# Loading queries and keys threefold and splitting them in place, in a kernel of one attention and two feed-forward stages

## The chip, the cores and the metric

The kernel runs on one core of one Trainium2 chip. The metric is the device time of one execution in microseconds (us). Five engines work side by side, each through its own instructions in order: TensorE (PE, with its weight loads PEld), VectorE (DVE), ScalarE (ACT), GpSimd (POOL), and SyncE (SP), which here only issues DMA transfers. An engine that reaches an instruction whose inputs are missing waits, and everything behind that instruction on the same engine waits with it.

## The reference

Inputs are q, k, v and o_gate (4 batches, 8 heads, 768 steps, 40 numbers a head) and two gates a step and head. For each batch and head a 40 by 40 state is carried over the 768 steps:

```python
m_new  = max(f_t + m, i_t)
f_stab = exp(f_t + m - m_new);  i_stab = exp(i_t - m_new)
C = f_stab * C + i_stab * outer(v_t, k_t)
n = f_stab * n + i_stab * k_t
y_t = sigmoid(o_t) * (C @ q_t) / max(|n . q_t|, 1)
```

The result, 3072 rows of 320, goes through two layers: `h = max(x@w1, x@w2, x@w3)` of width 768 and `h@w_out`; then `h = x@w_in` of width 2048, `g = h*clip(h+3, 0, 6)/6`, and `g@w_out`. Everything is float32. The weights come to the kernel as float64 numbers seen as int64.

## The kernel before

**Stages.** Stage 1 is attention with the first layer, stage 2 the second layer. Attention is cut into 24 groups: a group g is one batch and one chunk of 128 steps, all 8 heads (`attention(g)`, line 415). Groups 0 to 7 (g < GF = 8) are called early groups here, 8 to 23 late ones (the change's title counts them from 1). The first layer takes the groups in blocks of 2, 2 and five times 4 (BLK1), so its products (lines 284, 817, 819; tiles h and acc) run between the attention steps of later groups. Stage 2 (lines 930 to 1028) takes six blocks of 4 groups, and 16 slices k of its weights; a product into pi (line 284, called in g_in), then ACT, DVE, ACT and POOL steps (984 to 988), then products into po (1002 to 1004).

**Precision.** A product of float32 numbers is made as several products of rounded parts. A matrix x is split into hi, x rounded by a copy, and lo = x - hi. In the late groups queries and keys lie in a tile qs of 120 rows, three times 40: the rows of the queries are hi, hi, lo and those of the keys hi, lo, hi (or the same with the roles swapped), so that one product over 120 rows sums hi*hi, hi*lo and lo*hi. The state that the queries meet lies likewise in a tile cs of 120 rows.

**How a late group's qs is made.** Line 434 loads queries and keys once, 320 KB, into raw, a tile of 128 rows that has no regard to heads (raw has one buffer). ACT copies it to hi (sq, line 455), POOL subtracts to lo (sl, 458), SP writes both to a tensor qs_d in the chip's DRAM (sw, 464; 640 KB), and five more transfers (sr, 471, 473, 474; 960 KB) read it back into the rows of qs. The first of these steps waits for the product pv of the group AHEAD = 5 groups before.

**How the state's cs is made.** After the state cn of a group is there (line 705), ACT copies it to ch (709), POOL subtracts to cl (713), and six small transfers (cd, 720) put cl, ch and ch into the rows of cs. The product `in` (567) reads cs and qs.

**Weights of stage 1.** 24 pieces (`weights(k, p)`, line 732), each of 384 or 320 KB: SP loads it (wl, line 739, through load_f64, 246 to 249; four buffers wr), ACT reads its bytes twice (rebase 255, tail 263), DVE joins the two (267), ACT rounds (752), POOL subtracts (274). Both ACT steps read raw and so end the use of the buffer.

**Order.** Stage 1's steps are put to a planner (class Plan, 120). Each step is given an engine, a duration, a priority and what it reads and writes; the planner plays them through and writes each engine's order down. MOVED adds to the priority of single steps by their number, GP is the priority of the gates of chunks 1 to 5 and WP0, WPR that of the weights. SP's order comes from the same plan, so a transfer that must wait for a buffer holds up all that stand behind it on SP. Up to three PSUM tiles pa serve attention, two tiles h the first layer's inputs.

**Between the stages.** Each block of stage 1 writes its result x2 into x2_d in DRAM (xd, 850), two transfers a group; stage 2 reads it back likewise (x_load, 952).

Of the kernel before, what the change touches and what calls it, by code (L numbers as in the profile page):

```python
# [21 lines left out]
L = 128  # L22
# [4 lines left out]
QF = 2 * D * H * L // 128  # L27
FF1, FF2 = 768, 2048
K1, K2 = FF1 // 128, FF2 // 128
DP = 42  # L30
# [6 lines left out]
AHEAD, WP0, WPR = 5, 500, 100  # L37
GP, NSG = 1900, 4
GPB, GGB = 3, 4
PE_, PM, PC = 0, 2 * 10**6, 3 * 10**6  # L40

MOVED = {
    135: -1449, 206: -3641, 217: -1367, 319: 149, 371: 268, 387: 4201, 480: 39, 517: 2678, 522: 1135,
    539: 1040, 553: -4154, 559: -4352, 565: -156, 594: 613, 659: -1758, 707: -7, 715: 420, 742: -3344,
    940: 2702, 941: 5996, 953: 4436,
# [4 lines left out]
    qs=2, raw=1, sp=1, kvo=2, kvg=2, fd=2, vt=2, vw=2, nm=2, rr=2, y=2, sg=2, ct=1, cn=B + 1, ch=1, cl=1, cs=B + 1,  # L50
# [69 lines left out]
class Plan:  # L120
# [22 lines left out]
    def order(p):  # L143
# [17 lines left out]
        while ready:  # L161
            best = None
            for n in ready:
                o = p.ops[n]
                s = at[o["eng"]]
                for d in o["deps"]:
                    x = p.ops[d]
                    end = done[d]
                    if x["eng"] != o["eng"] or x["eng"] == "SP":
                        end += p.LAT.get(x["eng"], 0) + o["wait"]  # L170
                    s = max(s, end)
# [34 lines left out]
            if o["eng"] == "SP":  # L206
                dma = max(dma, s) + o["size"] / 210
                end = dma + 2000
# [16 lines left out]
def body(tc, ctx, qk0, qkf, kvo, ig, fg, w1, w2, out):  # L225
# [11 lines left out]
    qs_d = [dram.tile([2, 2, D, H * L], F32, name=f"qs_d{g}") for g in range(GF, G)]  # L237
    x2_d = [dram.tile([128, 3, L], F32, name=f"x2_d{g}") for g in range(G)]
# [7 lines left out]
    def load_f64(src, name):  # L246
        t = stg.tile([128, WC], I64, tag="wr", name=f"raw{name}", bufs=BUFS["wr"])[:, 0:src.shape[-1]]
        nc.sync.dma_start(t, src)
# [41 lines left out]
    with ExitStack() as c1:  # L290
# [14 lines left out]
        idt = cs1.tile([128, NC_, 2, BH], F32, name="idt")  # L305
        dL = cs1.tile([128, NC_ - 1, BH // 2], F32, name="dL")
        junk = cs1.tile([128, 512], BF16, name="junk")
# [4 lines left out]
        def gates(gp1, c0, c1_, pr):  # L312
# [71 lines left out]
            P.add("SP", 120, pr, load, w=[F, I], size=2 * 4 * w * BH)  # L384
# [30 lines left out]
        def attention(g):  # L415
# [7 lines left out]
            QS, FD, KVO = ("qs", g), [("fd", g, a) for a in range(2)], ("kvg" if g < 2 else "kvo", g)  # L423
# [3 lines left out]
            def lq():  # L427
# [16 lines left out]
            if g < GF:  # L444
                P.add("SP", 120, pr - 2100, lq, w=[QS], size=4 * 40 * 2048)
            else:
                P.add("SP", 60, pr - 4000, lq, r=[("pv", g - AHEAD)], w=[("raw", g)], size=4 * 128 * QF)
            P.add("SP", 60, pr - 2000, lk, w=[KVO], size=4 * 128 * 976)

            if g >= GF:  # L450
                d = qs_d[g - GF]

                def sq():
                    s["sp"] = sb("sp", g, [128, 2, QF], F32R)
                    nc.scalar.copy(s["sp"][:, 0], s["raw"])

                def sl():
                    nc.gpsimd.tensor_tensor(
                        out=s["sp"][:, 1], in0=s["raw"], in1=s["sp"][:, 0].bitcast(F32), op=ALU.subtract
                    )  # L460


                def sw():
                    nc.sync.dma_start(
                        d.rearrange("z a d n -> z (a d n)").rearrange("z (p f) -> p z f", f=QF), s["sp"].bitcast(F32)
                    )

                def sr():
                    s["qs"] = q = sb("qs", g, [120, 2, H, L], F32R)
                    q = q.bitcast(F32).rearrange("p a h t -> p a (h t)")  # L470
                    nc.sync.dma_start(q[0:D], d[0].rearrange("a d n -> d a n"))
                    for r, (zq, zk) in enumerate(((0, 1), (1, 0)), 1):
# [608 lines left out]
```

## Time and profile before

| | |
|---|---|
| median of 3 runs | 793.09 us (789.65 to 795.54) |
| profiled execution, its own time | 792.57 us |
| span from its first to its last instruction | 790.8 us |
| mean granted clock of TensorE | 0.956 |
| PE busy | 757.2 us (96%) |
| DVE, ACT, POOL busy | 400.6, 309.2, 423.3 us |
| moved by DMA | 92.65 MB |

The profile comes from one execution. It gives the busy time of each engine, in all and in slices of the span, the granted clock of TensorE (1.00 is 2.4 GHz, 0.50 is 1.2 GHz), and the waits, each put down to the event that came last before the engine went on. A busy PE need not work at its peak.

### The profile page before, as it was taken

The numbers are of one execution on the slowest core, as the hardware profiler recorded it, in microseconds if no ns is written. First come the engines' busy times: TensorE is split into PE (matmuls) and PEld (weight loads), VectorE is DVE, ScalarE is ACT, GpSimd is POOL, SyncE is SP. The second block draws the span as 40 slices with busy tenths as digits, with TensorE's granted clock in tenths as the row PEclk, the third lists the DMA queues.
The fourth block names the chain that finished last, engine by engine and source line by source line (L and its number), as shares of the span: only waits on it lengthen the run. The fifth ranks groups of instructions, "written<-read, shape, count | busy, mean of one in ns | idle before, by whom it ended". The sixth has DMA issues, their size and how long they took to land.

```text
span 790.8 us, 13152 instructions
## 1 busy us (share of the span) xinstructions
PE 757.2 (96%) x5063; PEld 661.8 (84%) x5063; DVE 400.6 (51%) x618; ACT 309.2 (39%) x597; POOL 423.3 (54%) x388
## 2 busy tenths in 40 slices
PE   8878969899999998999999999999999999999997
PEld 6768869788888787888888878898998899898986
DVE  5987738668868776578425665312212113121210
ACT  4585422222223122222415886634433334433432
POOL 3788737757768687573514456535334334333331
PEclk7689679999999999999999999999999999999999
DMA  8578567675657758743322642200100000000000
GB/s 260 164 242 273 162 170 200 161 239 178 199 175 212 228 158 246 233 148 84 112 59 76 202 157 72 68 1 10 59 1 0 34 1 1 34 1 1 34 1 34
DMA packets 52078, 92.65 MB, mean 117 GB/s; under 512 B 6032, under 2 KB 28528, under 8 KB 52016
## 3 DMA queue, kind: packets, MB, share of 16 engines
q1 hardware_dynamic: 52016, 91.82, 38.2%
q8 instruction: 40, 0.66, 0.3%
q14 instruction: 22, 0.18, 0.1%
HBM read 70.78 MB, written 18.43 MB: 113 GB/s over the span
## 4 chain that ended last, share of the span: by engine, by line
PE 60%; DMA 11%; ACT 5%; DVE 4%; POOL 4%; SPq 3%; issue 2%; POOLq 0%; ACTq 0%; DVEq 0%
PE pi L284 20%; PE h L284 13%; PE po L1003 6%; PE po L1002 6%; PE po L1004 6%; DMA qs<-qs_d 4%; PE acc L817 3%; DMA raw<-in_w 2%; DMA qs_d<-sp 2%; SPq L720 2%; DVE t L267 2%; PE sc L536 1%; DMA fd<-f_d 1%; ACT a L255 1%; PE acc L819 1%
## 5 line engine op out<-in xcount | busy, mean ns | idle before, releaser
L284 PE MATMUL h<-x,w 128*128 128x512 f32 (+1 forms) x1008 | 224.8, 374 | 6.7 <-ACT m L785 6.7
L988 POOL TENSOR_TENSOR gg<-r,gg 128x512 fp32r<-128x512 f32 x96 | 125.6, 1318 | 184.4 <-ACT gg L987 174.3
L284 PEld LDWEIGHTS h<-x,w 128*128 128x128 f32 x1008 | 175.7, 198 | 36.3 <-ACT m L785 8.1
L284 PE MATMUL pi<-xs,w 128*128 128x512 f32 x768 | 193.0, 395 | 1.5 <-ACT w L946 0.8
L985 DVE SCALAR_TENSOR_TENSOR r<-r,pi 128x512 f32<-128x512 f32 x96 | 64.3, 686 | 230.3 <-ACT r L984 230.1
L284 PEld LDWEIGHTS pi<-xs,w 128*128 128x128 f32 x768 | 140.8, 188 | 29.7 <-ACT w L946 1.1
L1002 PE MATMUL po<-w,gg 128*128 128x320 f32 x384 | 118.3, 310 | 1.1 <-ACT gg L987 0.5
L1003 PE MATMUL po<-w,gg 128*128 128x320 f32 x384 | 118.0, 309 | 0.0
L984 ACT ACTIVATE r<-pi,b 128x512 f32<-128x512 f32 x96 | 64.0, 687 | 133.8 <-PE pi L284 133.2
L1004 PE MATMUL po<-w,gg 128*128 128x320 f32 x384 | 111.2, 309 | 0.0
L801 POOL TENSOR_TENSOR hh<-m,hh 128x512 fp32r<-128x512 f32 (+1 forms) x42 | 51.1, 1216 | 70.2 <-ACT hh L797 68.9
L787 DVE TENSOR_TENSOR m<-h,m 128x512 f32<-128x512 f32 (+1 forms) x84 | 50.9, 606 | 63.6 <-PE h L284 51.2
L1002 PEld LDWEIGHTS po<-w,gg 128*128 128x128 f32 x384 | 72.1, 188 | 5.7 <-ACT gg L987 1.5
L817 PE MATMUL acc<-hh,w 128*128 128x512 f32 (+1 forms) x252 | 76.5, 382 | 0.0
L1003 PEld LDWEIGHTS po<-w,gg 128*128 128x128 f32 x384 | 72.1, 188 | 3.0
L987 ACT CAST gg<-r 128x512 fp32r<-128x512 f32 x96 | 59.0, 621 | 36.6 <-DVE r L985 34.4
L797 ACT CAST hh<-m 128x512 fp32r<-128x512 f32 (+1 forms) x42 | 23.5, 559 | 125.7 <-PE acc L817 117.2
L1004 PEld LDWEIGHTS po<-w,gg 128*128 128x128 f32 x384 | 70.4, 188 | 1.0 <-POOL gg L988 0.2
L274 POOL TENSOR_TENSOR w<-t,w 128x384 fp32r<-128x384 f32 (+2 forms) x46 | 49.0, 1073 | 22.0 <-ACT w L946 11.5
L506 DVE TENSOR_TENSOR_SCAN fd<-fd,ident 128x512 f32<-128x512 f32 x40 | 58.1, 1462 | 2.5 <-DMA fd<-f_d 2.5
L267 DVE SCALAR_TENSOR_TENSOR t<-a,t 128x384 uint32<-128x384 uint32 (+1 forms) x56 | 46.0, 840 | 15.6 <-ACT t L263 14.0
L817 PEld LDWEIGHTS acc<-hh,w 128*128 128x128 f32 x252 | 47.0, 200 | 6.3
(107 smaller groups left out, 971.9 us busy)
## 6 DMA issues: line engine op xcount, KB each, us to landing
raw<-in_w SPq DMA_DIRECT2D x34, 384.0 KB
kvo<-in_kvo SPq DMA_DIRECT2D x22, 488.0 KB
fd<-f_d SPq DMA_DIRECT2D x20, 512.0 KB
qs_d<-sp SPq DMA_DIRECT2D x16, 640.0 KB
qs<-qs_d SPq DMA_DIRECT2D x64, 160.0 KB
raw<-in_w SPq DMA_DIRECT2D x22, 320.0 KB
raw<-in_qkf SPq DMA_DIRECT2D x16, 320.0 KB
qs<-qs_d SPq DMA_DIRECT2D x16, 320.0 KB
```

The source lines that it names most:

```text
L267: nc.vector.scalar_tensor_tensor(out=t, in0=a.bitcast(U32), scalar=3, in1=t, op0=ALU.logical_shift_left, op1=ALU.bitwise_or)
L284: nc.tensor.matmul(ps, wt[:, a:a + 128], x[:, r], start=n == 0, stop=n == len(order) - 1)
L506: nc.vector.tensor_tensor_scan(out=half, data0=s.get(("bc", a), half), data1=ident4.rearrange("p h t -> p (h t)"), initial=0.0, op0=ALU.mu ...
L801: nc.gpsimd.tensor_tensor(out=t[:, 1], in0=T["m", j, k], in1=t[:, 0].bitcast(F32), op=ALU.subtract)
L817: nc.tensor.matmul(acc[a], wo[:, a * 128:128 + a * 128], h, start=first, stop=last)
L984: nc.scalar.activation(r, ps, AF.Relu, bias=b3)
L985: nc.vector.scalar_tensor_tensor(out=r, in0=r, scalar=6.0, in1=ps, op0=ALU.min, op1=ALU.mult)
L987: nc.scalar.copy(gg[:, 0], r)
L988: nc.gpsimd.tensor_tensor(out=gg[:, 1], in0=r, in1=gg[:, 0].bitcast(F32), op=ALU.subtract)
L1002: nc.tensor.matmul(po[t], hi, wo[:, 0:320], start=first, stop=False)
L1003: nc.tensor.matmul(po[t], hi, wo[:, 320:640], start=False, stop=False)
L1004: nc.tensor.matmul(po[t], lo, wo[:, 0:320], start=False, stop=last)
```

## The change

- A late group loads queries (a = 0) and keys (a = 1) from the inputs into two tiles raw of 120 rows, three transfers of 40 rows each (160 KB), six in all. raw has 2 buffers. The tensor qs_d, its write and its reads are gone.
- `hm`: ACT multiplies raw by a column `lows`, 1 in the rows that are to hold lo and 0 in the others, and rounds the result into sp, half of a tile (4 heads) at a time, four times a group. sp stays at one buffer, of 120 x 512 now. `ls`: raw - sp into qs, the queries' halves on DVE, the keys' on POOL; so a row holds lo where lows is 1 and hi where it is 0.
- Stage 1's weight loads are issued by ACT (`nc.scalar`), not SP.
- The state: ACT makes three copies of 40 x 168 into ch (two of them for the upper half), POOL subtracts straight into cs in two pieces, and two transfers instead of six fill the rest.
- x2_d is one tensor a block, written and read by two transfers a block.
- AHEAD is 6, GP 1055, cn and cs have one buffer less, durations given to the planner are larger for SP steps and some PE steps, a transfer's end counts 2.5 us after its bytes, and MOVED has some 170 entries instead of 21, so each engine's order in stage 1 is a new one.

```diff
-AHEAD, WP0, WPR = 5, 500, 100
-GP, NSG = 1900, 4
+AHEAD, WP0, WPR = 6, 500, 100
+GP, NSG = 1055, 4
+WLP, QLP = 800, 4000
...
-    qs=2, raw=1, sp=1, kvo=2, ... cn=B + 1, ch=1, cl=1, cs=B + 1,
+    qs=2, raw=2, sp=1, kvo=2, ... cn=B, ch=1, cs=B,
...
-            def lq():
+            def lq(a=0):
...
-                    s["raw"] = sb("raw", g, [128, QF])
-                    nc.sync.dma_start(s["raw"], qkf[g - GF])
+                    s["raw", a] = q = sb("raw", f"{g}_{a}", [120, H, L])
+                    for r in range(3):
+                        nc.sync.dma_start(q[r * D:r * D + D].rearrange("p h t -> p (h t)"), qkf[g - GF, :, a])
...
-                P.add("SP", 60, pr - 4000, lq, r=[("pv", g - AHEAD)], w=[("raw", g)], size=4 * 128 * QF)
+                for a in range(2):
+                    P.add("SP", 1100, pr - QLP + 400 * a, lambda a=a: lq(a), r=[("pv", g - AHEAD)], w=[("raw", (g, a))], size=120 * 4096)
...
-                def sq():
-                    s["sp"] = sb("sp", g, [128, 2, QF], F32R)
-                    nc.scalar.copy(s["sp"][:, 0], s["raw"])
-                def sl():
...
-                def sw():
...
-                def sr():
...
+                def hm(a, z):
+                    s["sp", a, z] = sb("sp", f"{g}_{a}{z}", [120, 4, L], F32R)
+                    x = s["raw", a][:, 4 * z:4 * z + 4]
+                    nc.scalar.activation(s["sp", a, z], x, AF.Copy, scale=lows[:, a:a + 1])
+                def ls(a, z):
+                    if "qs" not in s:
+                        s["qs"] = sb("qs", g, [120, 2, H, L], F32R)
+                    x = slice(4 * z, 4 * z + 4)
+                    eng = nc.gpsimd if a else nc.vector
+                    eng.tensor_tensor(out=s["qs"][:, a, x], in0=s["raw", a][:, x], in1=s["sp", a, z].bitcast(F32), op=ALU.subtract)
...
-            def ch():
-                s["ch"] = sb("ch", g, [128, 4, DP], F32R)
-                nc.scalar.copy(s["ch"], s["cn"])
+            def ch(r):
+                if "ch" not in s:
+                    s["ch"] = sb("ch", g, [128, H, DP], F32R)
+                x = slice(4 * r, 4 * r + 4)
+                for o in (0, 64)[0:r + 1]:
+                    nc.scalar.copy(s["ch"][o:o + D, x], s["cn"][64 * r:64 * r + D])
...
             def cd():
-                for n, x in enumerate(("cl", "ch", "ch")):
-                    for r in range(2):
-                        nc.sync.dma_start(
-                            t[n * D:n * D + D, 4 * r:4 * r + 4].bitcast(F32), s[x][64 * r:64 * r + D].bitcast(F32)
-                        )
+                for r in (D, 2 * D):
+                    nc.sync.dma_start(cs()[r:r + D].bitcast(F32), s["ch"][0:D].bitcast(F32))
...
             def wl():
-                s["raw"] = load_f64(w1[k, :, o:o + n], nm)
+                s["raw"] = load_f64(w1[k, :, o:o + n], nm, nc.scalar)
...
-            P.add("SP", 60, pr - 800, wl, w=[RAW], size=1024 * n)
+            P.add("ACT", 360, pr - WLP, wl, w=[RAW], size=1024 * n)
...
+        def low_rows():
+            for a, x in enumerate((2 * D, D)):
+                nc.vector.tensor_reduce(lows[:, a:a + 1], ident[0:120, x:x + D], axis=mybir.AxisListType.X, op=ALU.add)
```

## Rows read from the trace of the kernel before

**Rows 1.** The page's slices: busy tenths, granted clock, DMA share, each 19.8 us.
```profile
PE   8878969899999998999999999999999999999997
PEclk7689679999999999999999999999999999999999
DMA  8578567675657758743322642200100000000000
```

**Rows 2.** Busy time by stretch, us; then granted clock, DMA share and GB/s.
```profile
0.00:40.00 40.00, 34.92 (x217) 28.14 (x217) 29.77 (x50) 20.31 (x42) 21.10 (x29) 0.66 0.68 213
40.00:80.00 40.00, 32.56 (x297) 29.68 (x295) 31.90 (x56) 26.87 (x67) 32.96 (x37) 0.87 0.78 256
80.00:120.00 40.00, 32.11 (x250) 30.85 (x246) 22.07 (x42) 12.39 (x30) 22.65 (x25) 0.70 0.58 161
120.00:180.00 60.00, 57.94 (x531) 52.36 (x531) 43.30 (x75) 14.60 (x32) 41.66 (x44) 0.94 0.72 203
180.00:380.00 200.00, 196.78 (x1629) 164.44 (x1628) 148.51 (x231) 48.38 (x91) 136.28 (x130) 1.00 0.60 182
...
500.00:785.00 285.00, 285.00 (x1585) 257.11 (x1584) 60.67 (x83) 111.39 (x184) 112.58 (x84) 1.00 0.05 17
```

**Rows 3.** Timelines of ACT and PE, 88 to 110 us: in brackets idle time before, and what ended it.
```profile
88.25 0.56 ACT L263 ACTIVATE t<-raw 128x384 uint32<-128x384 uint8 x1 [2.97 <-POOL w L274]
...
105.91 0.54 ACT L255 ACTIVATE a<-raw 128x384 f32<-128x384 f32 x1 [12.27 <-DMA raw<-in_w]
...
107.83 2.08 PE L284 MATMUL h<-x,w 128*128 128x256 f32 x8 [6.11 <-ACT m L785]
```

**Rows 4.** Timeline of SP's queue, 85 to 100 us: what stood ahead of four weight loads.
```profile
85.45 1.54 SPq L720 DMA_DIRECT2D cs<-cl  x2
87.04 3.87 SPq L720 DMA_DIRECT2D cs<-ch  x4
91.03 0.41 SPq L498 DMA_DIRECT2D fd<-f_d  x1
...
94.05 5.50 SPq L248 DMA_DIRECT2D raw<-in_w  x4
```

**Rows 5.** Busy time by stretch around the long wait, columns as before.
```profile
88.00:91.00 3.00, 3.00 (x20) 2.92 (x19) 1.87 (x4) 2.12 (x5) 2.66 (x5) 0.50 0.12 32
...
88.00:100.00 12.00, 12.00 (x69) 11.75 (x68) 7.76 (x14) 4.77 (x11) 7.88 (x10) 0.50 0.69 180
...
99.60:104.60 5.00, 2.12 (x15) 1.92 (x14) 0.00 (x0) 0.00 (x0) 0.00 (x0) 0.84 1.03 158
```

**Rows 6.** Waits of SP's queue over the span: us in total, times, longest.
```profile
SPq L248 <- ACT t L263: 63.9, 29, 5.9
```

**Rows 7.** The chain of waits in order of time: pieces of transfers, start and length.
```profile
147.48 8.46 DMA qs<-qs_d
...
244.56 9.23 DMA qs_d<-sp
...
309.96 7.23 DMA qs<-qs_d
```

**Rows 8.** Groups of instructions by form: the removed ones and the nearest to the added.
```profile
L987 ACT CAST gg<-r 128x512 fp32r<-128x512 f32 x96 | 59.0, 621 | 36.6 <-DVE r L985 34.4 <-PE po L1004 2.2
L801 POOL TENSOR_TENSOR hh<-m,hh 128x512 fp32r<-128x512 f32 x30 | 41.6, 1388 | 53.4 <-ACT hh L797 52.4 <-DMA qs<-qs_d 1.0
L458 POOL TENSOR_TENSOR sp<-raw,sp 128x640 fp32r<-128x640 f32 x16 | 29.1, 1822 | 7.1 <-ACT sp L455 7.0
L593 DVE TENSOR_TENSOR pr<-fd 128x512 f32<-128x512 f32 x32 | 26.4, 838 | 0.5
L455 ACT CAST sp<-raw 128x640 fp32r<-128x640 f32 x16 | 11.7, 730 | 1.2 <-DMA qs_d<-sp 1.2
L713 POOL TENSOR_TENSOR cl<-cn,ch 128x168 fp32r<-128x168 f32 x16 | 10.9, 680 | 1.1 <-ACT ch L709 1.1
L709 ACT CAST ch<-cn 128x168 fp32r<-128x168 f32 x16 | 5.3, 332 | 10.0 <-DMA cs<-ch 5.7 <-DVE cn L705 4.3
```

**Rows 9.** One line's or tile's instructions: shortest, median and longest duration in ns.
```profile
L593 DVE TENSOR_TENSOR pr<-fd x32: 674/693/1809, 126.1 to 367.9; 128x512 f32<-128x512 f32 x32
...
L720 SPq DMA_DIRECT2D cs<-ch x64: 706/707/1622, 68.6 to 337.6; - x64
...
L248 SPq DMA_DIRECT2D raw<-in_w x56: 327/352/534, 4.1 to 478.2; - x56
```

**Rows 10.** Waits of PE between 40 and 380 us: us in total, times, longest.
```profile
PE h L284 <- ACT m L785: 6.7, 3, 6.1
PE sc L536 <- DVE nm L574: 2.7, 1, 2.7
PE sc L536 <- DMA cs<-ch: 2.2, 1, 2.2
...
PE sc L536 <- DMA qs<-qs_d: 2.1, 1, 2.1
PE dc L686 <- POOL vw L525: 1.9, 2, 1.8
```

More of the change, by code (lines that the diff above doesn't have):

```diff
@@ L422, in attention @@
             per_head = lambda x: x.unsqueeze(2).to_broadcast([128, H, DP])
-            QS, FD, KVO = ("qs", g), [("fd", g, a) for a in range(2)], ("kvg" if g < 2 else "kvo", g)
-            def lq():
+            QS, FD, KVO = [("qs", g, a, z) for z in range(2) for a in range(2)], [("fd", g, a) for a in range(2)], ("kvg" if g < 2 else "kvo", g)
+            def lq(a=0):
                 if g < GF:
@@ L450, in attention @@
+            P.add("SP", 360, pr - 2000, lk, w=[KVO], size=4 * 128 * 976)
             if g >= GF:
[L451 to L466 removed]
@@ new lines, in ls @@
+                def ls(a, z):
[4 more added lines that the diff above has]
+                    eng.tensor_tensor(out=s["qs"][:, a, x], in0=s["raw", a][:, x], in1=s["sp", a, z].bitcast(F32), op=ALU.subtract)
+                for z in range(2):
+                    for a in range(2):
+                        SPL, Q = ("sp", (g, a, z)), ("qs", g, a, z)
+                        P.add("ACT", 600, pr - QLP + 1000 + z, lambda a=a, z=z: hm(a, z), r=[("raw", (g, a)), ("lows",)], w=[SPL])
+                        P.add("POOL" if a else "DVE", 1220 if a else 600, pr - QLP + 1000 + z, lambda a=a, z=z: ls(a, z), r=[("raw", (g, a)), SPL], w=[Q])
@@ L576, in attention @@
                 nr = 2 if g < GF else 1
-                IN, ST = [("pa", f"in{g}_{r}") for r in range(nr)], ("cs" if g >= GF else "cn", g - B)
-                P.add("PE", 990, pr + 25, inter, r=[QS, ST], w=IN, wait=300)
+                IN, ST = [("pa", f"in{g}_{r}") for r in range(nr)], [("cs", g - B, r) for r in range(3)] if g >= GF else [("cn", g - B)]
+                P.add("PE", 990, pr + 25, inter, r=[*(QS if g < GF else QS[0:4:2]), *ST], w=IN, wait=300)
                 for r in range(nr):
@@ L851, in xd @@
                 x2 = T["x2", j]
-                for t, g in enumerate(range(*SP1[j])):
-                    nc.sync.dma_start(x2_d[g][:, 0:2], x2[:, 0:2, t * L:(t + 1) * L])
-                    nc.sync.dma_start(x2_d[g][0:64, 2], x2[0:64, 2, t * L:(t + 1) * L])
+                i, (a, e) = next((i, (a, e)) for i, (a, e) in enumerate(SP2) if a <= SP1[j][0] < e)
+                x = slice((SP1[j][0] - a) * L, (SP1[j][1] - a) * L)
+                nc.sync.dma_start(x2_d[i][:, 0:2, x], x2[:, 0:2])
+                nc.sync.dma_start(x2_d[i][0:64, 2, x], x2[0:64, 2])
             P.add("ACT", 130 + N, -1000, xo0, r=[A[2]], w=[X2[2]])
@@ L954, in x_load @@
             t = xr.tile([128, 3, NM2], F32, tag="xr", name=f"xr{j}")[:, :, 0:N]
-            for i, g in enumerate(range(*SP2[j])):
-                nc.sync.dma_start(t[:, 0:2, i * L:(i + 1) * L], x2_d[g][:, 0:2])
-                nc.sync.dma_start(t[0:64, 2, i * L:(i + 1) * L], x2_d[g][0:64, 2])
+            nc.sync.dma_start(t[:, 0:2], x2_d[j][:, 0:2])
+            nc.sync.dma_start(t[0:64, 2], x2_d[j][0:64, 2])
             return t
```

81 lines of the change are left out of this document (36 added, 45 removed), and 19 rows, old and new, of the table MOVED.

## The prediction

> **What bounds the kernel now.** I read the page's slices first [rows 1]. The reader is to see that PE is busy nearly everywhere, that its clock is below full in the first nine or so slices and nowhere else, and that DMA is busy in the first half alone. From 500 us on PE is busy 285.00 of 285 us at clock 1.00 [rows 2]: nothing that the change does can be felt there, and PE's own instructions are not changed. What can be gained lies in stage 1, as idle time of PE and as time at a lower clock. I count both for each stretch of [rows 2]: idle time is the length less PE's busy time, the clock's loss is the length times one less the granted clock (idle time at a low clock is counted in both, so the sums are upper ends).
>
> - 0 to 40 us: 5.1 idle, 40 x 0.34 = 13.6 by the clock.
> - 40 to 80: 7.4 and 40 x 0.13 = 5.2, together 12.6.
> - 80 to 120: 7.9 and 40 x 0.30 = 12, together 19.9; some 2 us are counted twice, so 18.
> - 120 to 180: 2.1 and 60 x 0.06 = 3.6. 180 to 380: 3.2 and none. Together 8.9.
>
> The worst place is 80 to 120 us. There PE stands still for 6.11 us until ACT has copied a product out (L785), and that copy stood on ACT behind a step that waited 12.27 us for a stage 1 weight [rows 3]. The clock is at its lower level, 0.50, from 88 to 100 us [rows 5]; PE had just been idle for 1.8 us waiting for vw [rows 10], and stays there through the long wait. The load itself was issued late: SP was busy with cs transfers from 85.45 to 90.9 us, then came fd, kvo and five reads of qs, and only at 94.05 four weight loads in a row [rows 4]. Meanwhile, from 88 to 91 us, the DMA engines were 0.12 busy; from 99.6 to 104.6 they were full at only 158 GB/s [rows 5]. So the weights waited for SP's order first, and for a queue of transfers afterwards.
>
> From 120 us on the chain of waits is full of the detour by qs_d: single pieces of 7 to 9 us, of which [rows 7] has three; the chain has some nine of over 3.6 us between 140 and 335 us. But PE loses only 8.9 us there, since the first layer's products fill in.
>
> **The change part by part.** All against the profiled execution's own 792.57 us, of which 1.8 us lie around the span; the median of the runs shown is 793.09, half a microsecond above.
>
> *Weight loads on ACT.* SP's queue waited 63.9 us in all, 29 times, for ACT to end its use of a weight buffer [rows 6] (stage 2's weights have a part in it), with everything else behind. Issued by ACT, a load needs no such wait, since ACT itself has just ended the use, and nothing of SP's stands ahead. In the case of [rows 4] the load would leave at 88.8, when ACT's step L263 on the old buffer is over [rows 3], instead of 94.05, into engines that are 0.12 busy. That takes away the 6.1 us of standing still, and with it a part of the low clock. Of the 18 us of this stretch I take 12; the lower bound is 3 (the weights still come late, and only the shorter queue helps), the upper 18. Between 40 and 80 us the loads stand in the same queue; of 12.6 us I take 3, bounds 0 and 6. The cost is 24 issues on ACT at 0.352 us [rows 9], 8.4 us in all, in a stretch in which ACT is busy 59.6 of 120 us [rows 2]; that is hidden as long as no copy L785 stands right behind one.
>
> The Trainium skill speaks against a part of this: "DMA: Bandwidth & Descriptors", section "Issuing engines are not separate DMA queues", says that transfers from any engine run on the same 16 DMA engines, and that a second issuing engine saves the issuing time alone. By that rule the burst of 91 to 107 us keeps its bytes and its length, this term is 3 instead of 12, and the forecast 9 us higher; by the row of 88 to 91 us the engines were free and the issue was what was late, so I stay with 12.
>
> *The detour by qs_d.* A late group loses 320 KB in, 640 KB out and 960 KB in again, and gains 6 x 160 = 960 KB: half the bytes, 15 MB over 16 groups, and a chain of load, split, write and read becomes load and split, requested six groups ahead. Late groups follow each other every 16 us or so; at the 158 GB/s of [rows 5] the new load takes 6.1 us of these. On SP six issues of 0.35 us take the place of seven, and two cs transfers that of six at 0.71 us [rows 9]. Of the 8.9 us after 120 us, with the two single waits of 2.2 and 2.1 us for cs and qs [rows 10], I take 5, bounds 0 and 8.
>
> *Added work.* ACT gets 64 steps hm near 0.621 us (39.7 us) for 16 of 0.730 (11.7), and 32 more small copies at 0.332 (10.6): 38.6 us more. DVE gets 32 subtractions at 0.838 us, 26.8 us. POOL gets 32 at 1.388 (44.4) for 16 at 1.822 (29.1) and 16 more small ones at 0.680 (10.9): 26.2 us more [rows 8]. Between 120 and 380 us that lifts DVE from 191.8 to some 215 of 260 us, POOL from 177.9 to 200, ACT from 63 to 97 [rows 2]. None becomes full, so it is hidden behind PE's products; but queues get longer, and PE's waits for DVE and POOL (2.7 and 1.9 us, [rows 10]) become more. I take 2 us; without that cover it would be all of DVE's 26.8, and with shorter queues elsewhere it could be 0.
>
> The durations of a subtraction from SBUF lie between 0.674 and 1.809 us [rows 9]: something holds it at times. The Trainium skill, "SBUF — State Buffer", section "Who interferes with whom", says that a VectorE instruction with two SBUF inputs and a GpSimd one that reads SBUF block each other in full; both halves of ls are of that kind. By the shortest duration DVE's part would be 21.6 us, by the mean, which has the blocking in it, 26.8; I used the mean.
>
> *The rest.* Merged x2_d transfers save 34 of 48 writes and 36 of 48 reads on SP; they lie beside full PE stretches, so nothing. The gates' earlier priority changes only when DVE takes them up; their exponentials wait for the sigmoids of groups 0 to 3 in any case (`after`, line 389). The new order as such I set at nothing, with 6 us either way: the trace of before can't show it.
>
> Sum: -12 - 3 - 5 + 2 = -18, so 774.6; against the median 775.
>
> **The rivals.**
>
> *A: the early stretch closes up more fully.* For it: the losses before 120 us are 18 + 12.6 + some 17, and a good part is one late stall pulling the next (clock 0.50 after an idle PE). With 4 us left of 12.6, 4 of 18, 2 of 8.9 and 5 less in the first 40 us: 8.6 + 14 + 6.9 + 5 less 2 is 32.5, giving 760. Against it: DVE is busy 31.9 of 40 us between 40 and 80 and ACT 26.9, so this stretch is also short of engines.
>
> *B: hidden anyway.* PE is nearly full from 120 us on, and the late weights are a matter of bytes, not of order; the rule on issuing engines above says the same. Then the terms are 3, 0 and 3, against 2: 788 to 789, no change that can be told. Against it is the idle DMA before the burst.
>
> *C: the one split buffer ties three engines together, slower.* sp has one buffer, so each of the four hm of a group waits until the subtraction before it has read it: ACT, POOL, ACT, DVE in turn, 64 turns. While ACT waits, its copies L785 and L797 stand behind it, and PE has but two tiles h. One turn held by one POOL step is 1.4 us; if a group's four turns cost PE 1.7 us together, that is 27 us, and with gains of 15 left from the first terms 792.6 - 15 + 27 = 804.6. It decides against the change from some 1.1 us a group on (17 us of gain over 16 groups). For it: one such hold shows in [rows 3], where PE stood 6.11 us behind ACT. Against it: ACT is idle for three quarters of the time after 120 us, and the split has several group times to spare, as loads are asked for six groups ahead.
>
> **How the numbers follow.** The forecast, 775, has 0.47, with its own range of 767 to 783; A 0.26 (760); B 0.13 (788); C 0.14 (805). The bound of what a measurement here can tell is 1%, 8 us. Faster by more: 0.47 + 0.26 = 0.73; within: 0.13; slower: 0.14. The range runs from 754, A with 6 us of the unknown order, to 797, B with the added work or the order 8 to 9 us dearer; C and a little of A's end lie outside.
>
> **What would show it.** Right: no ACT step of stage 1 waits over 3 us for a weight, clock above 0.85 between 80 and 120 us, DMA bytes near 77 MB, no transfer piece of qs over 5 us on the chain, first pi products some 15 us earlier, stage 2 unchanged in length. Wrong: a weight wait of 5 us or more remains (B), or waits of ACT's hm on DVE or POOL with PE idle behind L785 (C). A start below 0.66 clock in the first 40 us would speak against the order alone.

## The result, and the profile after

The changed kernel takes 803.14 us (median of 4 runs, 800.03 to 805.51) against 794.32 us (4 runs, 789.65 to 803.29) for the kernel before on the same chips. The ratio is 1.013 with a 95% interval from 1.0083 to 1.0177: it is slower, by about 1.3%, and outside the predicted range. The medians of the kernel before lay between 790.2 and 794.3 us beside the other kernels, so from here on small differences are read from ratios, and one per cent is about 8 us.

Its busy time by stretch (us, then PE, PEld, DVE, ACT, POOL with their numbers of instructions, granted clock, DMA share, GB/s):

```profile
0.00:40.00 40.00, 34.42 (x211) 22.51 (x211) 29.14 (x51) 20.42 (x43) 20.00 (x29) 0.74 0.65 202
40.00:80.00 40.00, 36.26 (x270) 33.99 (x270) 27.58 (x50) 25.11 (x62) 27.31 (x33) 0.71 0.75 227
80.00:120.00 40.00, 38.62 (x307) 36.43 (x307) 27.26 (x51) 18.86 (x44) 28.62 (x33) 0.79 0.50 163
120.00:180.00 60.00, 56.16 (x524) 49.12 (x526) 56.37 (x84) 23.34 (x47) 52.81 (x51) 0.97 0.47 141
180.00:380.00 200.00, 192.27 (x1542) 158.55 (x1543) 167.91 (x245) 77.22 (x144) 157.91 (x148) 0.98 0.39 125
...
500.00:785.00 285.00, 285.00 (x1573) 256.24 (x1573) 62.80 (x83) 113.08 (x186) 112.90 (x84) 1.00 0.05 17
```

Against [rows 2] the reader is to see two things. Up to 120 us PE is busier than before, 109.30 us in all against 99.59. From 120 us on the picture turns: DVE is busy 56.37 of 60 us where it was 43.30, POOL 52.81 where it was 41.66, and PE falls from 57.94 and 196.78 us to 56.16 and 192.27, its clock from 180 us on from 1.00 to 0.98.

A busy share of PE is a weak measure, since a product at half clock is busy for longer. The bracketed counts are a better one: they say how much of the fixed work is done. A record on a border counts in both stretches, so I count in one stretch from 0: at 120 us the kernel after has 787 matmul records and the kernel before 754, at 380 us they have 2849 and 2910. The kernel after is 33 ahead first, and then 61 behind. Some records can be missing, so this is a guide only.

What was moved went as forecast: DMA fell from 92.65 to 76.05 MB, and no step of ACT in stage 1 waits long for a weight. Two signs of being right are missing: the clock between 80 and 120 us is 0.79, not above 0.85, and the first product into pi starts at 394.7 us, after the 391.1 of before and not some 15 us ahead of it. The groups by form show what was added (partitions x elements, count, busy, mean ns, idle time before and its releaser):

```profile
L513 DVE TENSOR_TENSOR_SCAN fd<-fd,ident 128x512 f32<-128x512 f32 x40 | 62.8, 1584 | 3.1 <-DMA fd<-f_d 3.0
L480 POOL TENSOR_TENSOR qs<-raw,sp 120x512 fp32r<-120x512 f32 x32 | 47.6, 1488 | 15.8 <-ACT sp L473 15.4
L473 ACT ACTIVATE sp<-raw,lows 120x512 fp32r<-120x512 f32 x64 | 46.3, 724 | 76.7 <-DVE qs L480 25.1 <-POOL qs L480 23.3 <-DMA raw<-in_qkf 17.3
L816 POOL TENSOR_TENSOR hh<-m,hh 128x512 fp32r<-128x512 f32 x30 | 44.2, 1473 | 45.0 <-ACT hh L812 44.9
L480 DVE TENSOR_TENSOR qs<-raw,sp 120x512 fp32r<-120x512 f32 x32 | 31.8, 994 | 12.2 <-ACT sp L473 12.2
L600 DVE TENSOR_TENSOR pr<-fd 128x512 f32<-128x512 f32 x32 | 31.7, 997 | 1.3 <-PE pv L617 0.8
L654 POOL TENSOR_TENSOR y<-nm,sg 128x320 f32<-128x320 f32 x24 | 28.0, 1166 | 1.3
```

Two of their counterparts before, beside those of [rows 8]:

```profile
L506 DVE TENSOR_TENSOR_SCAN fd<-fd,ident 128x512 f32<-128x512 f32 x40 | 58.1, 1462 | 2.5 <-DMA fd<-f_d 2.5
L647 POOL TENSOR_TENSOR y<-nm,sg 128x320 f32<-128x320 f32 x24 | 23.1, 961 | 3.0 <-PE tr L656 1.3
```

The subtractions are 31.8 us on DVE and 47.6 on POOL, 5 and 3 us over their forecasts. But instructions that the change doesn't touch grew too: the scan of fd from 1462 to 1584 ns, pr from 838 to 997, y from 961 to 1166. DVE gained 32.5 us between 120 and 380 us (224.28 against 191.81), POOL 32.8.

Where this meets the path is seen in the chain of waits in order of time (start, us, what), pieces from the middle:

```profile
192.45 8.30 DMA raw<-in_qkf
...
225.62 1.43 DVE fd L513
227.04 2.13 DVE qs L480
...
230.24 2.15 DVE fd L513
...
235.20 0.73 POOL sg L649
236.00 1.15 POOL y L654
237.16 1.65 POOL vw L532
```

In [rows 7] the long pieces of this chain were transfers of qs_d. Now three loads of raw stand in it between 120 and 380 us (8.04, 8.30 and 3.44 us). For the most part it runs from one step of DVE or POOL to the next, in the order in which they stand on the engine, and the subtractions (qs, L480) stand among the steps that a group's products wait for.

The loads depend on the subtractions too. The two tiles of raw are those of one group, and the next group's loads need them free. These are waits of SP's queue for that (us in total, times, longest), with all that stands behind it on SP:

```profile
SPq L451 <- DVE qs L480: 48.4, 10, 8.5
SPq L451 <- POOL qs L480: 39.9, 13, 5.7
```

### The profile page after: what moved, and what is told of

It reads as the page before. It is cut to its first block, busy times and chain, and to the rows that moved or that the text cites. A ratio compares the mean times of both kernels' runs of the same rounds, so it can differ in the third digit from the quotient of the medians.

```text
span 799.1 us, 13173 instructions
## 1 busy us (share of the span) xinstructions
PE 769.1 (96%) x5082; PEld 663.8 (83%) x5082; DVE 434.8 (54%) x652; ACT 353.1 (44%) x677; POOL 459.3 (57%) x420
## 2 busy tenths in 40 slices
DMA packets 28655, 76.05 MB, mean 95 GB/s; under 512 B 3921, under 2 KB 9137, under 8 KB 28593
## 4 chain that ended last, share of the span: by engine, by line
PE 62%; DVE 13%; POOL 9%; ACT 7%; DMA 4%; issue 4%; SPq 0%; DVEq 0%; POOLq 0%; ACTq 0%
PE pi L299 20%; PE h L299 13%; PE po L1024 6%; PE po L1023 6%; PE po L1025 6%; PE acc L832 3%; DMA raw<-in_qkf 2%; POOL qs L480 2%; DVE qs L480 2%; DVE fd L513 2%; DVE t L282 2%; PE sc L543 2%; PE pv L611 1%; POOL hh L816 1%; DVE m L802 1%
## 5 line engine op out<-in xcount | busy, mean ns | idle before, releaser
L299 PE MATMUL h<-x,w 128*128 128x512 f32 (+1 forms) x1008 | 232.7, 383 | 5.8 <-POOL w L289 2.6
L299 PEld LDWEIGHTS h<-x,w 128*128 128x128 f32 x1008 | 179.2, 204 | 36.8 <-ACT m L800 3.8
L816 POOL TENSOR_TENSOR hh<-m,hh 128x512 fp32r<-128x512 f32 (+1 forms) x42 | 55.4, 1319 | 53.8 <-ACT hh L812 53.7
L473 ACT ACTIVATE sp<-raw,lows 120x512 fp32r<-120x512 f32 x64 | 46.3, 724 | 76.7 <-DVE qs L480 25.1
L289 POOL TENSOR_TENSOR w<-t,w 128x384 fp32r<-128x384 f32 (+2 forms) x46 | 45.0, 985 | 35.0 <-ACT w L767 23.9
L513 DVE TENSOR_TENSOR_SCAN fd<-fd,ident 128x512 f32<-128x512 f32 x40 | 62.8, 1584 | 3.1 <-DMA fd<-f_d 3.0
L480 POOL TENSOR_TENSOR qs<-raw,sp 120x512 fp32r<-120x512 f32 x32 | 47.6, 1488 | 15.8 <-ACT sp L473 15.4
```

Source lines behind the costliest of these rows:

```text
L299: nc.tensor.matmul(ps, wt[:, a:a + 128], x[:, r], start=n == 0, stop=n == len(order) - 1)
L480: eng.tensor_tensor(out=s["qs"][:, a, x], in0=s["raw", a][:, x], in1=s["sp", a, z].bitcast(F32), op=ALU.subtract)
L513: nc.vector.tensor_tensor_scan(out=half, data0=s.get(("bc", a), half), data1=ident4.rearrange("p h t -> p (h t)"), initial=0.0, op0=ALU.mu ...
L816: nc.gpsimd.tensor_tensor(out=t[:, 1], in0=T["m", j, k], in1=t[:, 0].bitcast(F32), op=ALU.subtract)
```

## The experiments

Eighteen kernels; the times are medians, the ratios are to the kernel before on the same chip.

| kernel | time, us | ratio to before, 95% interval |
|---|---|---|
| after | 803.14 | 1.013, 1.0083 to 1.0177 |
| a_copy: all 64 subtractions become copies on ACT | 781.78 | 0.9885, 0.9836 to 0.9934 |
| a_copy_dve: only DVE's 32 | 791.74 | 1.0032, 0.9999 to 1.0064 |
| a_copy_pool: only POOL's 32 | 788.66 | 0.999, 0.9962 to 1.0019 |
| a_inplace: hi written into qs, no sp | 813.99 | 1.0264, 1.0195 to 1.0333 |
| a_nosub: no subtraction, ACT writes qs | 795.02 | 1.0019, 0.9979 to 1.0059 |
| a_nosub_dve: the same for DVE's half alone | 804.27 | 1.0126, 1.0049 to 1.0204 |
| a_w_sp: weights back on SP | 797.46 | 1.0048, 1.0001 to 1.0095 |
| b_w_act: before, weights on ACT | 794.6 | 1.0029, 0.999 to 1.0069 |
| a_nomoved: after, MOVED empty | 823.55 | 1.0419, 1.0345 to 1.0492 |
| b_nomoved: before, MOVED empty | 775.95 | 0.9838, 0.9797 to 0.988 |
| an_copy: a_copy, MOVED empty | 786.48 | 0.9954, 0.9921 to 0.9988 |
| an_w_sp: a_w_sp, MOVED empty | 818.18 | 1.0352, 1.0271 to 1.0433 |
| bn_w_act: b_nomoved, weights on ACT | 776.53 | 0.9823, 0.9758 to 0.9889 |
| bn_x2: b_nomoved, merged x2_d | 776.47 | 0.9809, 0.9746 to 0.9872 |
| bn_cs: b_nomoved, the new way to cs | 776.93 | 0.9813, 0.976 to 0.9867 |
| c_80: one load, split in 80 rows | 795.81 | 1.0047, 1.0012 to 1.0082 |
| f_all: no split at all | 786.28 | 0.9956, 0.9931 to 0.9981 |
| f_all0: f_all, MOVED empty | 794.77 | 1.0056, 1.0029 to 1.0082 |

### The turns over sp, or the work itself?

Two theories stood first: that the one buffer sp makes three engines take turns (the prediction's rival C), and that the subtractions' work on DVE and POOL is what costs. For turns speak ACT's waits in the group of L473 above: 25.1 us for DVE's and 23.3 for POOL's reading of sp. The first test takes sp away, hi going straight into qs and the subtraction working in place:

```diff
-                    s["sp", a, z] = sb("sp", f"{g}_{a}{z}", [120, 4, L], F32R)
+                    if "qs" not in s:
+                        s["qs"] = sb("qs", g, [120, 2, H, L], F32R)
+                    s["sp", a, z] = s["qs"][:, a, 4 * z:4 * z + 4]
```

> The changed kernel, but ACT's rounded copy goes straight into qs and the subtraction works there in place, so the one split buffer and the turns taken over it are gone; steps, columns and each engine's order stay. Theory work (the added subtractions fill DVE and POOL between 120 and 380 us): within 4 us of the changed kernel's 803, DVE still near 56 and POOL near 53 of 60 us busy between 120 and 180. Theory turns (the one buffer ties ACT, DVE and POOL together): 795 or below, the 48 us of ACT's waits for subtractions gone, PE's loss between 120 and 380 us down by half.

It became slower, 813.99 us. The test isn't clean: hm now needs a free qs, which sp let it do without, and up to 120 us PE is busy 100.56 us where the kernel after has 109.30. From 120 to 380 us, where nothing of the early loads is left, PE is busy 246.88 us (after: 248.43), so with the turns over sp gone nothing came back there. The next two leave subtractions out, with the same flaw; in a_nosub_dve the condition is `a in (0,)`:

```diff
+                    if a in (0, 1):
...
+                        nc.scalar.activation(s["qs"][:, a, 4 * z:4 * z + 4], x, AF.Copy, scale=lows[:, a:a + 1])
+                        return
```

> The changed kernel without the subtractions of queries and keys (all three parts of qs hold what ACT rounds, so the low parts are missing); ACT's 64 steps and all loads stay. Theories work and turns: 792 or below, DVE and POOL each some 25 to 45 us less busy before 380 us. Theory order (the new order and the first 120 us make the loss): 799 or above.

> As the run without subtractions, but only the queries' subtractions, those on DVE, are left out; the keys' stay on POOL with the split buffer. If DVE is the engine that decides: 795 or below, most of what leaving out all of them gives. If POOL decides: 800 or above.

795.02 (between the cases expected) and 804.27 us: between 120 and 380 us PE is busy 257.71 and 252.85 us against 248.43, but both lose before 120 us what a_inplace lost (103.27 and 101.20 us). The flaw is the same in a_inplace and a_nosub, and neither has turns over sp: they differ by the subtractions alone, and by 1.0264 - 1.0019 = 2.45% (19 us). Their stretches from 120 to 380 us, a_inplace first:

```profile
120.00:380.00 260.00, 246.88 (x2065) 208.02 (x2063) 226.67 (x325) 98.82 (x194) 210.42 (x199) 0.98 0.42 131
120.00:380.00 260.00, 257.71 (x2229) 219.34 (x2229) 195.88 (x318) 102.47 (x201) 166.66 (x177) 1.00 0.42 135
```

A fourth kernel is without the flaw: it keeps sp and the moment at which qs is first needed, and puts a copy by ACT in the place of each subtraction, which leaves the low parts out. Here the turns between engines go as well, since ACT now both fills sp and reads it:

```diff
-                    eng = nc.gpsimd if a else nc.vector
-                    eng.tensor_tensor(out=s["qs"][:, a, x], in0=s["raw", a][:, x], in1=s["sp", a, z].bitcast(F32), op=ALU.subtract)
+                    nc.scalar.copy(s["qs"][:, a, x], s["sp", a, z].bitcast(F32))
```

> The changed kernel with the 64 subtractions of queries and keys replaced by 64 copies on ACT, from the split buffer into qs (the low parts are missing); DVE and POOL lose these steps, qs is still taken only at the second step, so unlike the run without subtractions the early loads of qs should not be held up. Theory work (DVE and POOL are full between 120 and 380 us): 791 or below, PE's loss in that stretch down by 10 us or more, and the first 120 us as in the changed kernel. Theory order: 799 or above.

781.78 us, 2.45% of before's time or 20 us less than the kernel after. Its stretches from 120 us on, and its scan and y:

```profile
120.00:180.00 60.00, 59.13 (x568) 52.41 (x565) 46.89 (x82) 35.35 (x72) 42.52 (x47) 1.00 0.51 161
180.00:380.00 200.00, 199.14 (x1613) 165.33 (x1612) 142.29 (x228) 104.32 (x188) 126.11 (x128) 1.00 0.40 128
```

```profile
L512 DVE TENSOR_TENSOR_SCAN fd<-fd,ident 128x512 f32<-128x512 f32 x40 | 54.8, 1386 | 4.2 <-DMA fd<-f_d 4.1
L653 POOL TENSOR_TENSOR y<-nm,sg 128x320 f32<-128x320 f32 x24 | 23.6, 982 | 1.5
```

DVE is back at 46.89 and POOL at 42.52 of 60 us, PE is full again at clock 1.00, the scan is down from 1584 to 1386 ns and y from 1166 to 982. ACT does 39.6 us more work, and no wait of PE for it shows below. (In the first 40 us, before any hm, this execution ran at clock 0.87 where the kernel after had 0.74; that isn't the subtractions' doing.) The waits of PE between 120 and 380 us (in total, times, longest), after (but for four rows of 0.2 to 0.6 us) and then in a_copy:

```profile
PE sc L543 <- POOL qs L480: 3.0, 2, 2.3
PE h L299 <- ACT m L800: 2.0, 3, 0.9
PE in L574 <- DVE qs L480: 1.9, 2, 1.3
PE tr L663 <- POOL y L654: 1.4, 2, 1.1
PE dc L693 <- POOL vw L532: 1.2, 2, 0.9
PE dc L693 <- DVE fd L547: 0.7, 1, 0.7
...
```

```profile
PE pv L616 <- POOL pr L604: 0.8, 1, 0.8
PE pi L299 <- ACT w L967: 0.5, 1, 0.5
PE tr L662 <- POOL y L653: 0.3, 1, 0.3
```

After, they come to 11.6 us with the four, of which 9.4 are for DVE and POOL; in a_copy to 1.6. The subtractions themselves (qs) are 4.9 of the 9.4; the rest is for steps that were there before. With a_inplace and a_nosub, which have no turns on either side, the loss is put down to the subtractions on DVE and POOL. How much of it comes straight from the added work on the two engines, and how much by way of the late loads of raw, no run separates: without subtractions raw comes free sooner too (in a_copy SP waits 41.6 us for ACT to free it, instead of 88.3).

One engine at a time tells whether the two hold each other up:

> The changed kernel, in which only VectorE's 32 subtractions (the queries' half) are replaced by ScalarE copies of the rounded part; the low parts of the queries are left out. With all 64 replaced the kernel took 781.8 us, 21 less than the changed kernel. Theory 1 (each engine's own work counts, since both are nearly full between 120 and 180 us): VectorE's half brings about half of it, 790 to 794 us. Theory 2 (what counts is that a VectorE and a GpSimd instruction with two operands from SBUF hold each other up): taking away either half removes the collision, so most of the 21 us comes back, 783 to 787 us, and GpSimd's remaining 32 subtractions fall from a mean of 1.49 us to 1.25 or less. Theory 3 (GpSimd is the engine that is late): 798 to 803 us.

> The changed kernel, in which only GpSimd's 32 subtractions (the keys' half) are replaced by ScalarE copies of the rounded part; the low parts of the keys are left out. Theory 1 (own work of each engine): 790 to 794 us. Theory 2 (they hold each other up): 783 to 787 us, and VectorE's remaining subtractions fall from a mean of 0.99 us to about 0.7, the state gates' scan from 1.58 to 1.46 us. Theory 3 (GpSimd is the late engine): 782 to 786 us, with VectorE's durations hardly shorter.

DVE's half alone brings 0.98% (8 us), POOL's alone 1.4% (11 us), both 2.45%: the parts add up, as theory 1 says, POOL's a little more than it expected. The subtractions that stay, in a_copy_pool and in a_copy_dve:

```profile
L483 DVE TENSOR_TENSOR qs<-raw,sp 120x512 fp32r<-120x512 f32 x32 | 31.7, 991 | 5.1 <-ACT sp L473 4.9
```

```profile
L483 POOL TENSOR_TENSOR qs<-raw,sp 120x512 fp32r<-120x512 f32 x32 | 43.3, 1353 | 9.1 <-ACT sp L473 8.7
```

DVE's take 991 ns without POOL's and 994 with them; POOL's fall from 1488 to 1353 without DVE's. If a mutual block were what costs, taking either half away would have brought most of the 20 us back, and it didn't. The neighbours share the gain: the scan is at 1470 ns in a_copy_pool and 1483 in a_copy_dve.

### The weight loads

```diff
-                s["raw"] = load_f64(w1[k, :, o:o + n], nm)
+                s["raw"] = load_f64(w1[k, :, o:o + n], nm, nc.scalar)
```

> The kernel before with one thing of the change, stage 1's weight loads issued by ACT at their old places in the order. By the prediction's first term: 780 or below, the long wait at 94 to 106 us gone. By the result of putting them back on SP in the changed kernel (797 for 803): 797 or above, the loads taking their share of the DMA engines from the loads that attention needs in the first 60 us.

> The changed kernel with stage 1's weight loads issued by SP again, at the same places of the order. If the loads on ACT gained what the page shows between 80 and 120 us (7 us less lost than before): 808 or above, with a long wait of ACT for a weight. If they only cost, by crowding the gates' small loads in the first 5 us: 800 or below, and the first scan starts near 3.1 us instead of 4.8.

Put alone into the kernel before, the edit brings nothing (1.0029), and the long wait is still there, in the timeline of ACT:

```profile
108.45 0.49 ACT L255 ACTIVATE a<-raw 128x320 f32<-128x320 f32 x1 [8.98 <-DMA raw<-in_w]
```

One row of the kernel before says why, and I had not read it: that of the last step that ACT does for stage 1's weights, the rounding.

```profile
L752 ACT CAST w<-t x24: 442/511/514, 16.8 to 90.7; 128x384 fp32r<-128x384 f32 x18, 128x320 fp32r<-128x320 f32 x6
```

All 24 roundings are over at 91.2 us, and their 24 loads had landed before. The four loads at 94.05 us [rows 4] and the step that waited 12.27 us for one [rows 3] belong to stage 2 (`w2_prep`), whose loads the change leaves on SP.

Taken out of the kernel after, the edit gives 0.8% back (797.46 us; its interval and that of the kernel after overlap, so it may be less). The start of ACT's timeline, after and in a_w_sp:

```profile
0.81 1.86 ACTq L263 DMA_DIRECT2D raw<-in_w  x4
...
5.92 0.31 ACT L406 ACTIVATE gf<-gf 32x128 f32<-32x128 f32 x1 [1.93 <-DVE gf L350]
...
9.46 0.35 ACTq L263 DMA_DIRECT2D raw<-in_w  x1
9.86 0.18 ACT L395 COPY idt<-gps 128x32 f32<-128x32 f32 x1 [2.56 <-DMA raw<-in_w]
9.94 0.51 ACT L767 CAST w<-t 128x384 fp32r<-128x384 f32 x1
```

```profile
4.13 0.31 ACT L406 ACTIVATE gf<-gf 32x128 f32<-32x128 f32 x1 [2.04 <-DVE gf L350]
...
6.61 0.19 ACT L395 COPY idt<-gps 128x32 f32<-128x32 f32 x1 [0.68 <-PE gps L391]
6.70 0.51 ACT L767 CAST w<-t 128x384 fp32r<-128x384 f32 x1
```

On ACT the four first loads leave at once and the gates' exponentials come 1.8 us later; then the fifth load's issue at 9.46 stands on ACT ahead of the copy of idt, which was ready, and the first weight is rounded 3.2 us later. By 120 us a_w_sp has 857 matmul records, after 787.

### The order

```diff
-MOVED = { ... }
+MOVED = {}
```

> The changed kernel with an empty MOVED, so in the planner's own order. If the new order is what makes the changed kernel slow: 800 or below. If the order earns something and the added work makes the loss: 812 or above.

> The kernel before, without its 21 hand-set offsets of priorities (the list of moves is empty), all else as it was. In the changed kernel, emptying its list cost 20 us. If the old list did as much for the old kernel, 810 to 816 us; if the two lists differ in worth, because the new one is much longer, 796 to 802 us, and then 10 to 20 us of the changed kernel's loss are hidden by its better order.

This was the surprise. Without its list the kernel after loses 2.9% (20 us); the kernel before gains 1.6% (14 us, its 790.23 in that comparison against 775.95), and with 775.95 us it is the fastest of all that ran. So before and after stand at orders of very different worth, and the prediction compared a kernel that its list holds back with one that its list helps. Its stretches:

```profile
0.00:40.00 40.00, 34.76 (x216) 28.11 (x217) 29.92 (x51) 20.47 (x42) 21.26 (x29) 0.66 0.68 215
40.00:80.00 40.00, 35.20 (x309) 32.51 (x308) 34.07 (x57) 28.70 (x70) 35.17 (x40) 0.83 0.69 213
80.00:120.00 40.00, 37.84 (x336) 36.32 (x336) 25.85 (x53) 14.87 (x38) 24.71 (x30) 0.91 0.81 250
120.00:180.00 60.00, 58.62 (x556) 50.24 (x554) 47.67 (x76) 13.96 (x29) 47.77 (x48) 1.00 0.66 205
180.00:380.00 200.00, 197.55 (x1574) 165.05 (x1573) 145.43 (x226) 52.45 (x98) 134.18 (x124) 1.00 0.61 184
```

Most of the gain is where the prediction looked for it: 37.84 us busy and clock 0.91 from 80 to 120 us, against 32.11 and 0.70 in [rows 2]; from 40 to 80 us PE is 2.6 us busier too. The same detour by qs_d is in it.

So the parts were measured once more on the planner's own order, where neither kernel has a list:

> The changed kernel with its list of offsets emptied (823.6 us), and with all 64 subtractions replaced by ScalarE copies; the low parts of the late groups' queries and keys are left out. If the added work on VectorE and GpSimd is what costs, whatever the order, the saving is 21 us or more: 795 to 803 us. If the subtractions cost only because the hand-set order puts them in the way, the saving is under 10 us: 814 to 824 us.

> The changed kernel with its list of offsets emptied (823.6 us), and stage 1's weight loads issued by SP. If issuing on ScalarE costs by itself (late first loads of the gates, copies held behind an issue), 4 to 8 us less: 815 to 820 us. If the 6 us seen with the hand-set order were that order's: 821 to 826 us.

> The kernel before with its list of offsets emptied (776.0 us), and stage 1's weight loads issued by ScalarE. If the prediction's term is right after all (the loads are late on SP's queue), 3 us or more less: 765 to 773 us. If the queue doesn't matter: 774 to 778 us. If issuing on ScalarE costs: 779 to 785 us.

> The kernel before with its list of offsets emptied (776.0 us), and the outputs of stage 1 written and read in one pair of transfers a block in place of one a group. The prediction's term: nothing, 774 to 778 us. If the 70 issues on SP held up loads behind them: 770 to 773 us.

> The kernel before with its list of offsets emptied (776.0 us), and the changed kernel's way to a late group's state: three small ScalarE copies and two GpSimd subtractions in place of one each, and two transfers inside SBUF in place of six. If the transfers' issues on SP (four fewer of some 0.7 us for each of 16 states) were worth more than the added work: 768 to 773 us. If the added work on GpSimd and ScalarE (10.9 and 10.6 us) is felt as the subtractions are: 778 to 785 us. If neither counts: 774 to 778 us.

There the whole change takes the kernel from 775.95 to 823.55 us, 5.8% of before's time or 46 us. The subtractions are 4.65% of it (37 us, more than the 21 to 29 that were expected), the weights on ACT 0.7% (5 us; the two intervals overlap, but the size is that of a_w_sp). Weights on ACT, merged x2_d and the new cs, each put alone into b_nomoved, bring and cost nothing (776.5, 776.5, 776.9), each inside what was expected for that case. The added work of the new cs, some 11 us each on POOL and ACT, costs nothing there. If the parts add up, some 0.5% is left for the rest: the end of the detour, the planner's constants, the earlier and longer loads, one buffer less of cn and cs; these weren't tried alone. The subtractions' price in the stretch from 180 to 380 us, in a_nomoved and then in an_copy:

```profile
180.00:380.00 200.00, 180.33 (x1466) 148.69 (x1466) 169.06 (x244) 71.56 (x132) 160.97 (x147) 0.95 0.41 126
```

```profile
180.00:380.00 200.00, 195.91 (x1556) 163.72 (x1555) 146.57 (x223) 99.11 (x178) 123.29 (x122) 0.99 0.39 126
```

90 more products in the same 200 us. SP waits only 29.4 us for subtractions in a_nomoved, against 88.3 in the kernel after, and yet they cost more there: the late loads of raw can't be all of the price. By the records up to 380 us these kernels stand as by time: a_nomoved 2796, after 2849, before 2910, an_copy 2931, a_copy 2972, b_nomoved 2982. (a_inplace has 2753 with 814 us, fewer than a_nomoved with 824, so the count isn't exact.)

### Other ways to do without the detour

c_80 loads a late group once, 80 rows, splits it there (half as many steps as in 120 rows) and fills qs by six transfers inside SBUF:

```diff
-                    for r in range(3):
-                        nc.sync.dma_start(q[r * D:r * D + D].rearrange("p h t -> p (h t)"), qkf[g - GF, :, a])
+                    nc.sync.dma_start(q.rearrange("p h t -> p (h t)"), qkf[g - GF])
...
+                    for r in range(3):
+                        if r == 2 - a:
+                            nc.sync.dma_start(q[r * D:r * D + D, a], s["raw"][a * D:a * D + D])
+                        else:
+                            nc.sync.dma_start(q[r * D:r * D + D, a], s["sp"].bitcast(F32)[a * D:a * D + D])
```

> A third way to qs: the changed kernel with weights on SP, but queries and keys loaded once into 80 rows, split there (ACT rounds, DVE and POOL subtract in place, half the columns of the changed kernel), and six transfers from SBUF to SBUF put the parts into qs; 480 KB less through DRAM than before, half the added work; one buffer more for cn and cs. Theory work: PE's loss between 120 and 380 us under 18 us and the time under 795. If the chain of transfers decides instead: 800 or above, with PE waiting for transfers into qs.

795.81 us, half a per cent over before and less than the kernel after, and between the two cases expected; weights on SP, cn and cs with their old buffers, and an order that wasn't made for it. a_w_sp, with the whole of the added work and weights on SP, is as fast (1.0048 against 1.0047), so halving the work brought nothing that shows here; whether the order or the transfers took it back, no run separates. f_all splits nothing: all groups go the way of the early ones, in 16 products of 40 rows each for scores and state.

```diff
-NBC, GF, G3 = 4, 8, 8
+NBC, GF, G3 = 4, 24, 8
```

> A version that might beat both: all 24 groups are treated as the first 8 are, their queries and keys loaded once in float32 and multiplied in plain float32 (16 products of 40 rows instead of 8 of 120 for the scores of a group, the same for the state's part), so that nothing is split, rounded or written to DRAM for groups 9 to 24; weights back on SP's queue, three buffers of qs, an order of its own. TensorE has some 0.25 us of scores and 0.29 us of state products more in each of 16 groups by their durations in the profile, about 9 us, and ScalarE, VectorE and GpSimd have some 40, 27 and 44 us less than in the changed kernel. If VectorE's and GpSimd's work is what the changed kernel lost its time by: 785 to 793 us, with VectorE at most 43 of 60 us between 120 and 180. If TensorE's added 9 us are felt in full and nothing else was late in the kernel before: 797 to 806 us.

> The version with all groups in plain float32 (786.3 us with offsets found by the planner's model), with no offsets at all. If a hand-set order pays only where the model is right, and the model was as wrong here as for the kernel before: 770 to 780 us. If its offsets do what they do for the changed kernel: 800 to 810 us.

786.28 us, a ratio of 0.9956: a gain, inside what was expected, though DVE is busy 52.40 of 60 us between 120 and 180 where I had expected at most 43. What fills it there was not followed up. Without a list it is 794.77 us, which neither case expected, so its list earns 8. It moves 63.85 MB and is still 10 us slower than b_nomoved, which has all the transfers of the kernel before.

## Why the prediction was wrong

**The step that failed first is the added work: "None becomes full, so it is hidden behind PE's products ... I take 2 us".** The amounts were nearly right (DVE and POOL were to reach 215 and 200 of 260 us and reached 224 and 211; hm took 724 ns, not 621). The reading was wrong: an engine needn't be full to cost. From 180 to 380 us DVE is at 0.84 and POOL at 0.79, and PE stands still for 7.7 us where it had been 3.2. Nor does added work spread evenly: from 120 to 180 us, where DVE and POOL had been near their mean (0.72 and 0.69), 13 and 11 us more brought them to 0.94 and 0.88. A group's products wait for a row of short steps that go from DVE to POOL and back, and each of them stands behind whatever is on its engine. The price is 20 us by a_copy in the kernel's own order, 37 us in the planner's, against 2; the bound named for it, "all of DVE's 26.8", was the nearer end, and the planner's order passes even that, since POOL's work counts as well.

**The weight loads: -12 and -3.** The long wait was for a stage 2 weight, whose loads the change doesn't touch. That the stretch had something to give is borne out by b_nomoved, in which the wait is gone and which is 14 us faster; but its order differs in other stretches too, so the size of the term isn't shown. In the kernel after the wait is gone as well, and in a_w_sp, so not by the moved loads. The clock was misread: it didn't stay low through the wait, [rows 5] has 0.84 from 99.6 to 104.6 us. And ACT's issues aren't free of waits, as the fifth load shows. The edit alone gives 0 (b_w_act, bn_w_act); in the kernel after it costs 5 to 6 us. The Trainium skill's "DMA: Bandwidth & Descriptors", section "Issuing engines are not separate DMA queues", which I had weighed and set behind the trace, was the better guide: a second issuing engine saves the issuing time alone, and here nothing came of it. The cost that is seen is the engine's own steps held behind an issue (2.56 us at 9.86).

**The detour: -5.** The bytes fell as computed, and the long pieces of qs_d left the chain. But loads of raw of over 8 us took their place: "requested six groups ahead" didn't hold, since raw has room for one group and comes free only after its subtractions. No time came from that which a run shows: b_nomoved keeps the whole detour and is the fastest, and an_copy, which has neither detour nor subtractions, is 10 us slower than it (some 5 of these may be the weights on ACT, by an_w_sp). In the hand-set order a_copy is 1.15% faster than before; whether that is the detour's, the new list's or the low parts' that it leaves out, no run separates.

**The order: 0 with 6 us either way.** The list of the kernel before costs it 1.6%, that of the kernel after saves 2.9%. The 1.3% measured is what is left of 5.8% for the change on the planner's own order (1.0419 and 0.9838, 5.8 apart) less 2.9 and 1.6.

**The rest** (merged x2_d, cs) at nothing was right on the planner's own order: 776.5 and 776.9 against 776.0.

**The rivals.** C's time, 805, was near, and its sign: it was the only case on this side. That was luck, as its mechanism isn't what the runs bear out. ACT does wait for the turns over sp, 48.4 us together, but a_inplace without sp recovers nothing from 120 us on, and from a_inplace to a_nosub, with no turns on either side, the subtractions cost the same 2.45% as from the kernel after to a_copy. Of its test, "PE idle behind L785" (L800 now), the waits above have 2.0 us of 11.6. They are many and short, none over 2.3 us, where the rival had looked for one hold a group.

## What to carry to other kernels

Before work is put on an engine "off the path", don't take a busy share below 1 for room. If steps that the bottleneck waits for run on the same engine, ask what the work will stand in front of, and take its whole duration for the possible price: the subtractions, 32 us on DVE and 48 on POOL, cost 20 and 37 us, while the 11 us of the new cs on POOL cost nothing. Ask also which buffer the new work frees, and which transfer waits for that. Ask of every wait on which a gain rests whose operation it is, and whether the change touches that very one: the row of the operation by line, with its count and its last start, answers it. And where an order is hand-set, measure both kernels without the list as well: otherwise the lists are compared along with the change.

## What the runs showed of the hardware

- Instructions that nothing was done to grew by 8 to 21% when DVE and POOL got fuller: the scan 1462 to 1584 ns, pr 838 to 997, y 961 to 1166. With copies on ACT in the subtractions' place the scan was at 1386, below the kernel before. It isn't so for each: on the planner's order pr took 993 ns with the subtractions and 1006 without. The Trainium skill's "SBUF — State Buffer", section "Who interferes with whom", says that a VectorE instruction with two SBUF inputs contends with a GpSimd one that reads SBUF. The growth fits that, but no run shows it to be the cause; of the subtractions themselves, DVE's were as long without POOL's (991 ns) as with them (994), while POOL's were shorter without DVE's (1353 against 1488).
- ACT took on 39.6 us of copies (618 ns each) in a_copy without a cost that shows: between 180 and 380 us it was busy 104.32 of 200.
- A transfer's issue on an engine that computes is a step like others: a ready copy stood 2.56 us behind it.
